# Holding back two decay loads, spreading one norm, joining state masks and moving the mix's scratch in a fused scan and feed-forward kernel

## The chip, the cores and the metric

The kernel runs on one core of a Trainium2 chip, as one launch. The metric is the device time in microseconds (us); lower is better. TensorE (PE) multiplies matrices, VectorE (DVE) and ScalarE (ACT) work elementwise, GpSimd (POOL) has little to do here, and transfers are issued from two queues: SyncE's (SP) and ScalarE's own. Each engine runs its instructions strictly in the order in which the program gives them.

## What is computed

Three stages follow one another: a decaying linear attention (a scan over the sequence), a gated feed-forward with RMS norm, and a second feed-forward that mixes each token with the one before it.

```python
# stage 1: per batch, head; state carried over the sequence
y_i   = sum_{j<=i} (C_i . B_j) * exp(cum_i - cum_j) * x_j + exp(cum_i) * (C_i . state)
state = exp(cum_last) * state + sum_j exp(cum_last - cum_j) * B_j x_j
# stage 2: x = y as (3072 tokens, 256)
xn = x / sqrt(mean(x*x) + 1e-6) * rms_g
x  = (silu(xn @ w_gate) * (xn @ w_val)) @ w_out          # 256 -> 1536 -> 256
# stage 3: per batch of 768 tokens, prev = the token before
xk, xr = mu_k*x + (1-mu_k)*prev, mu_r*x + (1-mu_r)*prev
out = sigmoid(xr @ w_r) * (relu(xk @ w_k)**2 @ w_v)      # 256 -> 1024 -> 256
```

Sizes: 4 batches, 8 heads, 768 positions, head size 32, state size 16.

## The kernel before

**Tiles.** The sequence is cut into six tiles of 128 positions; a tile holds the 4 batches, so 512 columns. For tile t the loop at L993 runs the first feed-forward (`ffn1`, twelve units of 128 hidden columns) and then, behind it, the second feed-forward of tile t-1 (`ffn2`, eight units). Each product of full precision is three matmuls of rounded parts (`mm3`, L748 to L750). In between, hooks weave in the attention of tile c = t+1, and loads for tile e = t+2. The hook "ab" runs ahead of each unit of `ffn1`, the hook "cd" ahead of each unit of `ffn2`.

**Attention of a tile c > 1.** A tile E of decays per batch (128x1024, 4 buffers) is loaded as factors by `load_e` (L332, on ACT's queue, 512 KB each) and turned into running products by `e_scan` (L501, DVE). `terms` (L425 to L433) builds the factors Bs and Cs of a batch's scores with ACT and DVE, and then loads the inputs Br and Cr of the batch after the next (L418, SP's queue). `masked` multiplies scores by decays (L514). `ch_mul` (L496, DVE) scales Ch, which `load_ch` fetches (L320, SP). `y_four` multiplies all out (L594, L527, L533), copies the result yT with ACT, and updates the state (`st_up` L615) and its masked copy Sf (`sf_up` L620), batch by batch. Right behind it stand the four loads of the E tiles for e. Tile 1 does the same in two halves, by `y_two`.

**The norm.** `rms_sq`, `rms_mm`, `rms_a` form the factors; `rms_b` (L711, L712, L720) spreads them over the rows; `xn_f` (L730) multiplies and `xn_split` rounds into two parts (L140 ACT, L143 DVE). For tile 1 all that is needed before its first `ffn1` unit.

**The mix.** `mix` (L809) needs a scratch tile p1 twice per tile. It has the tag "wt", one buffer, which the converted weights of every second pair and, from tile 2 on, the unit output sl use too. The tag "Cs", one buffer too, is that of the terms Cs and of the other converted weights.

**Order.** The program's text gives only ranks. `arrange` (L1357) runs a list scheduler over all instructions with a cost for each, gives each engine the instruction of the lowest rank that is ready and whose buffers are free, and fixes that order. Buffers of a tag are given out in the order in which the text first touches them (`can`, L1265). Instructions under `soonest` are urgent: nothing long is started right ahead of them. `chains` adds an edge of order between two instructions. Weights are converted during tiles 0 and 1 (L268 to L289), on DVE and ACT.

**Semaphores of transfers.** The framework hands eight completion semaphores to the transfers in turn, over both queues, and a transfer waits until the eighth before it has landed. At the end of tile 1's `ffn1` the order is Cr, Ch, E, E, x, E, three decay loads, E: the fourth E load is the eighth after Ch.

Of the kernel before, what the change touches and what calls it, by code (L numbers as in the profile page):

```python
# [13 lines left out]
AF = mybir.ActivationFunctionType  # L14
ALU = mybir.AluOpType

P = 128
NB, NH, S, D, N = 4, 8, 768, 32, 16
NC = S // P
# [5 lines left out]
M8 = 8  # L25
# [4 lines left out]


SCORES = ((4, 7), (3, 8), (2, 4, 8, 10))
VALUES = ((5, 7, 8, 10), (4, 6, 9, 11), (9, 10, 11, 12))
SCAN = ({3: (4,)}, {0: (0,), 1: (4, 1), 3: (2,), 5: (3,)})

NEED = ((4, 6, 8, 8, 10, 12, 12, 14, 16, 16, 18, 18, 18),
# [5 lines left out]
LOW_POOL, ON_POOL = (), ()  # L42

SUB_DVE, MIX_UNIT = tuple(range(27)), 9
MEANS = (7, 10)
WARM, COLD, HALVED, FILL = (9,), 11, 2, {('n', 0): 1, ('n', 2): 1}

TABLES = {AF.Ln: "natural_log_exp_and_others", AF.Exp: "natural_log_exp_and_others",
# [29 lines left out]
def tile_kernel(ctx: ExitStack, tc, a_c, x_t, B_t, B_s, C_s, B_p, C_p, C_h, kc,  # L78
# [116 lines left out]

    def decays(a_sb):
        a_r = t2("a_r")[:NC * NR]
        nc.vector.tensor_copy(a_r, a_sb)
        nc.vector.memset(a_r.rearrange("p (h i) -> p h i", h=4)[:, :, 0:1], 0.0)
        nc.sync.dma_start(out=rows4(la_r.rearrange("c b h i -> (c b h i)")), in_=a_r)  # L200
        nc.sync.dma_start(out=rows4(la_d.rearrange("c b h i -> (c b h i)")), in_=a_sb)
# [127 lines left out]

    def load_e(c, b):  # L330
        e = A[c]["E", b] = rp.tile([P, NH, P], F32, tag="E", bufs=4, name="E")
        nc.scalar.dma_start(  # L332
            out=e.rearrange("p h i -> p (h i)"),
            in_=la_r[c, b].rearrange("h i -> (h i)").unsqueeze(0).broadcast_to([P, NH * P]),
        )

# [224 lines left out]
    def y_two(c, b):  # L563
        d = A[c]
        y = [patt.tile([P, T], F32, tag="at", name="y") for _ in range(2)]
        for k in range(2):
            for half in range(2):
                g = slice(64 * half, 64 * half + 64)
                mm = nc.tensor.matmul(y[half][:, k * P:(k + 1) * P], Sf[g, b + k].rearrange("p h d -> p (h d)"),
                                 d["Ch"][g, b + k, :], start=k == 0, stop=False, skip_group_check=True)  # L570
                if k + half == 0:
                    groups.append((mm.ins.name, [t.name for t in y]))
        for k in range(2):
            y_x(y, (k * P, k * P), c, b + k, False)
            if c + 1 < NC:
                d["up", b + k] = y[k][:, 2 * P:2 * P + 2 * D]
                y_st(d["up", b + k], c, b + k)
        if b == 0:
            d["yT"] = rp.tile([P, 2, T], F32, tag="yT", bufs=1, name="yT")
        for half in range(2):  # L580
            nc.scalar.copy(d["yT"][:, half, b * P:(b + 2) * P], y[half][:, :2 * P])
        for k in range(2):
            st_up(c, b + k)
            sf_up(c, b + k)

    def y_four(c):
        d = A[c]
        y = [patt.tile([P, T], F32, tag="at", name="y") for _ in range(2)]
        more = c + 1 < NC
        u = pmm.tile([P, T], F32, tag="mm", name="u") if more else None  # L590
        for b in range(NB):
            for half in range(2):
                g = slice(64 * half, 64 * half + 64)
                mm = nc.tensor.matmul(y[half][:, b * P:(b + 1) * P], Sf[g, b].rearrange("p h d -> p (h d)"),  # L594
                                      d["Ch"][g, b, :], start=b == 0, stop=False, skip_group_check=True)
                if b + half == 0:
                    groups.append((mm.ins.name, [t.name for t in y + [u] * more]))
        for b in range(NB):
            y_x(y, (b * P, b * P), c, b, False)
            if more:  # L600
                d["up", b] = u[:, 2 * D * b:2 * D * (b + 1)]
                y_st(d["up", b], c, b, True)
        d["yT"] = rp.tile([P, 2, T], F32, tag="yT", bufs=1, name="yT")
        for half in range(2):
            nc.scalar.copy(d["yT"][:, half], y[half])
        for b in range(NB):
            st_up(c, b)
            sf_up(c, b)

    def st_up(c, b):  # L610
        if c + 1 >= NC:
# [3 lines left out]
        nc.vector.scalar_tensor_tensor(out=st, in0=st, scalar=A[c]["la"][:, b, P:P + 1], in1=u,  # L615
                                       op0=ALU.mult, op1=ALU.add)

    def sf_up(c, b):
        if c + 1 < NC:
            nc.vector.tensor_mul(  # L620
                Sf[:, b].rearrange("p (h j) d -> p h j d", j=2),
                state[:, b].unsqueeze(1).broadcast_to([P, NH // 4, 2, D]),
                k_sb[:, M8:M8 + NH // 2].rearrange("p (h j) -> p h j", j=2).unsqueeze(3).broadcast_to([P, NH // 4, 2, D]))


    spans = {}
# [182 lines left out]
    def mix(t, x2, he, le):  # L809
        def seq(ap):  # L810
            return ap.rearrange("p (b i) -> p b i", b=NB)

        last, new = carry[0], rp.tile([P, 2, NB], F32, tag="carry", bufs=2, name="carry")
        carry[0] = new

        def mixed(j, m, p1):
            f = t2("xf")
            if t == 0:
                nc.scalar.activation(out=p1, in_=x2[m][:, :, 1:], func=AF.Copy, scale=mu_v[j][:, m:m + 1])
                nc.vector.scalar_tensor_tensor(out=seq(f), in0=x2[m][:, :, :P], scalar=om_v[j][:, m:m + 1],  # L820
                                               in1=seq(p1), op0=ALU.mult, op1=ALU.add)
                return f
            nc.scalar.activation(out=p1, in_=x2[m], func=AF.Copy, scale=mu_v[j][:, m:m + 1])
            nc.vector.scalar_tensor_tensor(
                out=seq(f)[:, :, 1:], in0=seq(x2[m])[:, :, :P - 1], scalar=om_v[j][:, m:m + 1],
                in1=seq(p1)[:, :, 1:], op0=ALU.mult, op1=ALU.add)
            nc.vector.scalar_tensor_tensor(
                out=seq(f)[:, :, 0], in0=last[:, m, :], scalar=om_v[j][:, m:m + 1],
                in1=seq(p1)[:, :, 0], op0=ALU.mult, op1=ALU.add)
            return f  # L830

        for m in range(2):
            nc.vector.tensor_copy(new[:, m, :], x2[m][:, :, P] if t == 0 else seq(x2[m])[:, :, P - 1])
        for j in range(2):
            p1 = t4("p1")
            fs = [mixed(j, m, p1[:, m, :]) for m in range(2)]
            x = quad("xm")
            for m in range(2):
                xm[t, j, m] = x[:, m]
                split(x[:, m], fs[m], he, le)  # L840

    def ffn2(t, hook):
        acc = [None, None]
# [9 lines left out]
        for u in range(NK):  # L853
            hook("cd", u)
            kp = pmm.tile([P, T], F32, tag="mm", name="kp")
            for k in range(2):
                mm3(kp, wk, k, u, xm[t, 0, k], k == 0, k == 1)
            if u == 0:
                hook("cd2", u)
            rl, k2 = t2("rl"), t2("k2")  # L860
            nc.scalar.activation(out=rl, in_=kp, func=AF.Relu)  # L861
            if t == 0:
                nc.scalar.activation(out=k2, in_=rl, func=AF.Square)
            else:
                nc.vector.tensor_mul(k2, rl, rl)  # L865
            hs[u] = pair("hl", "h2")
            split(hs[u], k2, act_e, vec_e)
            if u >= 3:
                contract(u - 3)
# [123 lines left out]
    for t in range(NC):  # L993
# [11 lines left out]
        def finish(b):  # L1005
            if c > 1:
                if b == NB - 1:
                    y_four(c)
                    for k in range(NB):
                        if e < NC:  # L1010
                            load_e(e, k)
            elif b % 2:
                y_two(c, b - 1)
                for k in range(b - 1, b + 1):
                    if e < NC:
                        load_e(e, k)
# [3 lines left out]
        def attend(u):  # L1020
# [30 lines left out]
            if t == 0:  # L1051
                if u == MEANS[0]:
                    rms_sq(c, cols[0], act_e, vec_e)
                if u == MEANS[0] + 1:
                    rms_mm(c, cols[0])
                if u == MEANS[1]:
                    rms_sq(c, cols[1], act_e, vec_e)
                    rms_mm(c, cols[1])
                    soonest(rms_a, c, full)

        def hook(kind, u):
            if kind == "ab":
                if t == 0:
                    need(NEED[0][u])
                    if u == 0:
                        for b in range(NB):
                            sf_up(0, b)
                if t == 1:
                    need(NEED[1][u])
                    if u == MIX_UNIT:  # L1070
# [7 lines left out]
            if kind == "cd" and c < NC:  # L1078
# [12 lines left out]
                        e_scan(e, 1)  # L1091
                elif u == 6:
                    xn_out(c, (1,), full, act_e, vec_e)

        x2, tail = ffn1(t, hook)
        if t == 0:
            tail()
            hook("ab", NU)
            soonest(rms_b, c, full)
            soonest(xn_out, c, range(2), full, act_e, vec_e)  # L1100
            x2s = quad("x2s", F32).rearrange("p i a n -> p (i a n)")[:, :2 * NB * (P + 1)]
            x2s = x2s.rearrange("p (m b i) -> p m b i", m=2, b=NB)
            nc.gpsimd.memset(x2s[:, :, :, 0:1], 0.0)
# [301 lines left out]
```

## Time and profile before

| | us |
|---|---|
| median of 3 runs | 513.17 (512.85 to 513.82) |
| profiled execution | 516.1 |
| its span | 514.1 |
| TensorE busy in the span | 503.5 (98%) |
| VectorE busy | 377.5 (73%) |
| ScalarE busy | 307.1 (60%) |

The profiled execution is 2.9 us longer than the median of the runs, and 2.0 us of its time lie outside the span. The busy time of TensorE counts pipelined matmuls and says little about its pace; what counts is the distance between the starts of two matmuls in the timeline, 0.23 us for a 128x512 one.

### The profile page before, as it was taken

The numbers are of one execution on the slowest core, as the hardware profiler recorded it, in microseconds if no ns is written. First come the engines' busy times: TensorE is split into PE (matmuls) and PEld (weight loads), VectorE is DVE, ScalarE is ACT, GpSimd is POOL, SyncE is SP. The second block draws the span as 40 slices with busy tenths as digits, with TensorE's granted clock in tenths as the row PEclk, the third lists the DMA queues.
The fourth block names the chain that finished last, engine by engine and source line by source line (L and its number), as shares of the span: only waits on it lengthen the run. The fifth ranks groups of instructions, "written<-read, shape, count | busy, mean of one in ns | idle before, by whom it ended". The sixth has DMA issues, their size and how long they took to land.

```text
span 514.1 us, 7506 instructions
## 1 busy us (share of the span) xinstructions
PE 503.5 (98%) x2869; PEld 407.6 (79%) x2869; DVE 377.5 (73%) x625; ACT 307.1 (60%) x508; POOL 9.5 (2%) x26
## 2 busy tenths in 40 slices
PE   8999999999979999999999999999999999999996
PEld 4687777888858888888888888888888888888885
DVE  6899999979689783759995659996537763335662
ACT  5997778568369753556763546754448642246551
POOL 1000000000010000010000010000001000000000
PEclk9999999999989999999999999999999999999999
DMA  7958565342440111161102143001000010000101
GB/s 258 283 161 271 167 238 195 115 133 83 96 170 0 63 42 41 45 221 63 41 22 82 42 145 122 22 23 40 0 1 1 0 41 3 0 1 0 41 1 41
DMA packets 23283, 42.60 MB, mean 83 GB/s; under 512 B 3136, under 2 KB 6720, under 8 KB 23248
## 3 DMA queue, kind: packets, MB, share of 16 engines
q1 hardware_dynamic: 20496, 33.41, 19.6%
q10 hardware_dynamic: 2752, 8.72, 5.2%
q8 instruction: 22, 0.36, 0.3%
q14 instruction: 13, 0.11, 0.1%
HBM read 38.52 MB, written 3.34 MB: 81 GB/s over the span
## 4 chain that ended last, share of the span: by engine, by line
PE 87%; DVE 7%; DMA 3%; ACT 1%; issue 1%; DVEq 0%; ACTq 0%
PE v L748 10%; PE v L749 10%; PE v L750 10%; PE g L748 6%; PE g L749 6%; PE x L748 6%; PE g L750 6%; PE x L749 6%; PE x L750 5%; PE kp L748 4%; PE kp L749 4%; PE kp L750 4%; PE y L527 2%; DMA Ch<-in_C_h 2%; PE sc L476 1%; DMA E<-la_r 1%
## 5 line engine op out<-in xcount | busy, mean ns | idle before, releaser
L792 DVE TENSOR_TENSOR hf<-sl,v 128x512 f32<-128x512 f32 x72 | 49.1, 684 | 48.2 <-PE v L750 46.9
L140 ACT CAST h<-hf 128x512 fp32r<-128x512 f32 x72 | 44.2, 618 | 64.0 <-DVE hf L792 63.8
L133 ACT ACTIVATE sl<-g 128x512 f32<-128x512 f32 x72 | 42.5, 593 | 46.5 <-PE g L750 40.7
L143 DVE TENSOR_TENSOR h<-hf,h 128x512 fp32r<-128x512 f32 x72 | 50.3, 702 | 26.7 <-ACT h L140 26.6
L748 PE MATMUL x<-h,woh 128*128 128x512 f32 x144 | 56.7, 397 | 3.5 <-ACT h L140 3.1
L748 PE MATMUL g<-xn,wgh 128*128 128x512 f32 (+1 forms) x148 | 57.9, 391 | 0.3 <-ACT wgh L288 0.2
L748 PE MATMUL v<-xn,wvh 128*128 128x512 f32 (+1 forms) x148 | 56.9, 384 | 0.5 <-ACT sl L133 0.5
L749 PE MATMUL x<-h,wol 128*128 128x512 f32 x144 | 56.9, 395 | 0.4 <-DVE wol L289 0.4
L749 PE MATMUL g<-xn,wgl 128*128 128x512 f32 (+1 forms) x148 | 57.0, 385 | 0.0
L749 PE MATMUL v<-xn,wvl 128*128 128x512 f32 (+1 forms) x148 | 56.9, 384 | 0.0
L750 PE MATMUL g<-xn,wgh 128*128 128x512 f32 (+1 forms) x148 | 56.8, 384 | 0.0
L750 PE MATMUL v<-xn,wvh 128*128 128x512 f32 (+1 forms) x148 | 56.8, 384 | 0.0
L750 PE MATMUL x<-h,woh 128*128 128x512 f32 x144 | 56.1, 394 | 0.0
L140 ACT CAST h<-k 128x512 fp32r<-128x512 f32 x48 | 29.7, 620 | 17.8 <-DVE k L865 17.6
L143 DVE TENSOR_TENSOR h<-k,h 128x512 fp32r<-128x512 f32 x48 | 32.8, 687 | 10.0 <-ACT h L140 9.7
L865 DVE TENSOR_TENSOR k<-rl 128x512 f32<-128x512 f32 x40 | 29.1, 727 | 14.9 <-ACT rl L861 14.8
L748 PE MATMUL kp<-xm,wkh 128*128 128x512 f32 x96 | 38.0, 396 | 0.0
L749 PE MATMUL kp<-xm,wkl 128*128 128x512 f32 x96 | 37.6, 392 | 0.0
L750 PE MATMUL kp<-xm,wkh 128*128 128x512 f32 x96 | 37.5, 391 | 0.0
L748 PE MATMUL v<-h,wvvh 128*128 128x512 f32 x96 | 37.4, 389 | 0.0
L749 PE MATMUL v<-h,wvvl 128*128 128x512 f32 x96 | 37.3, 389 | 0.0
L501 DVE TENSOR_TENSOR_SCAN E<-E,cmask 128x1024 f32<-128x1024 f32 x16 | 36.6, 2285 | 0.9 <-DMA E<-la_r 0.9
(157 smaller groups left out, 979.6 us busy)
## 6 DMA issues: line engine op xcount, KB each, us to landing
E<-la_r ACTq DMA_DIRECT2D x16, 512.0 KB
x<-in_x_t SPq DMA_DIRECT2D x6, 512.0 KB
wst<-in_w_gate SPq DMA_DIRECT2D x6, 512.0 KB
wst<-in_w_val SPq DMA_DIRECT2D x6, 512.0 KB
wst<-in_w_out SPq DMA_DIRECT2D x6, 512.0 KB
Br<-in_B_s SPq DMA_DIRECT2D x12, 256.0 KB
Cr<-in_C_s SPq DMA_DIRECT2D x12, 256.0 KB
out<-r SPq DMA_DIRECT2D x11, 256.0 KB
```

The costliest lines, as they stand in the source:

```text
L133: one = nc.scalar.activation(out=out, in_=in_, func=func, **kw).ins.name
L140: last[1] = nc.scalar.copy(x[:, 0, :], src).ins
L143: last[0] = le.tensor_tensor(out=x[:, 1, :], in0=src, in1=f32(x[:, 0, :]), op=ALU.subtract).ins
L476: mm = nc.tensor.matmul(banks[j // 2][j % 2][:, k * w:(k + 1) * w], br[g, k * P:(k + 1) * P], cr[g, k * w:(k + 1) * w], start=True, stop=True)
L501: nc.vector.tensor_tensor_scan(out=e, data0=e, data1=cmask, initial=0.0, op0=ALU.mult, op1=ALU.max)
L527: nc.tensor.matmul(y[half][32 * j:32 * j + 32, at[half]:at[half] + P], x[:, b, h * D:(h + 1) * D], m[:, h, :], start=start and at[half] == ...
L748: nc.tensor.matmul(ps[:, s], w[0][:, k, ws], x[:, 0, s], start=first, stop=False, skip_group_check=s.stop - s.start < T)
L749: nc.tensor.matmul(ps[:, s], w[1][:, k, ws], x[:, 0, s], start=False, stop=False, skip_group_check=s.stop - s.start < T)
L750: nc.tensor.matmul(ps[:, s], w[0][:, k, ws], x[:, 1, s], start=False, stop=last, skip_group_check=s.stop - s.start < T)
L792: nc.vector.tensor_mul(hf, sl, v)
L865: nc.vector.tensor_mul(k2, rl, rl)
```

## The change

- `load_e`: behind `y_four` only the loads of batches 0 and 1 are issued. Those of batches 2 and 3 stand ahead of units 3 and 6 of `ffn2`, each behind the last Relu issued before it (`marks`). Still on ACT's queue. Tile 1's `y_two` keeps its loads, two behind each half.
- `mix`: p1 has the tag "Cs" in place of "wt".
- `sf_up`: one instruction for 4 (or 2) batches in place of one for each, behind all the state updates.
- `decays`: the copy of the 48x512 decays is made by ACT in place of DVE.
- Tile 0: the first half of tile 1's attention is finished ahead of unit 6 in place of 7 (`VALUES`), the first squares of the norm stand at unit 6 in place of 7 (`MEANS`), and `rms_b` and `xn_f` ahead of unit 11 (`SPREAD`) in place of behind the last unit; only `xn_split` stays there.

```diff
-VALUES = ((5, 7, 8, 10), (4, 6, 9, 11), (9, 10, 11, 12))
+VALUES = ((5, 6, 8, 10), (4, 6, 9, 11), (9, 10, 11, 12))
-MEANS = (7, 10)
+MEANS, SPREAD, LOAD_E = (6, 10), 11, (3, 6)
     def decays(a_sb):
-        nc.vector.tensor_copy(a_r, a_sb)
+        nc.scalar.copy(a_r, a_sb)
     def y_two(c, b):
         for k in range(2):
             st_up(c, b + k)
-            sf_up(c, b + k)
+        sf_up(c, b, 2)
     def y_four(c):
         for b in range(NB):
             st_up(c, b)
-            sf_up(c, b)
+        sf_up(c, 0, NB)
     def mix(t, x2, he, le):
-            p1 = t4("p1")
+            p1 = t4("p1", tag="Cs")
     def ffn2(t, hook):
-            nc.scalar.activation(out=rl, in_=kp, func=AF.Relu)
+            marks.append(nc.scalar.activation(out=rl, in_=kp, func=AF.Relu).ins.name)
     def finish(b):
                     y_four(c)
-                    for k in range(NB):
+                    for k in range(2):
                         if e < NC:
                             load_e(e, k)
 # ahead of units of ffn1, tile 0
+                if u == SPREAD:
+                    soonest(rms_b, c, full)
+                    for half in range(2):
+                        soonest(xn_f, c, half, full)
 # hook "cd", ahead of unit u of ffn2
+                if u in LOAD_E and e < NC:
+                    chains.append((marks[-1], load_e(e, 2 + LOAD_E.index(u))))
 # behind ffn1 of tile 0
-            soonest(rms_b, c, full)
-            soonest(xn_out, c, range(2), full, act_e, vec_e)
+            for half in range(2):
+                soonest(xn_split, c, half, full, act_e, vec_e)
```

## Rows read from the trace of the kernel before

**Rows 1.** The page: busy time and count of each engine; the chain by engine.
```profile
PE 503.5 (98%) x2869; PEld 407.6 (79%) x2869; DVE 377.5 (73%) x625; ACT 307.1 (60%) x508; POOL 9.5 (2%) x26
PE 87%; DVE 7%; DMA 3%; ACT 1%; issue 1%; DVEq 0%; ACTq 0%
```

**Rows 2.** The chain that ended last, 134 to 147 us: start, length, engine, line.
```profile
134.77 8.05 DMA Ch<-in_C_h
...
143.88 1.28 ACT L125
145.17 1.06 ACT sq L662
...
146.79 0.63 PE x L748
```

**Rows 3.** Timeline of PE: start, length, line, operation, count, idle before and its releaser.
```profile
143.07 0.39 PE L749 MATMUL x<-h,wol 128*128 128x512 f32 x1
143.29 0.39 PE L750 MATMUL x<-h,woh 128*128 128x512 f32 x1
146.79 0.63 PE L748 MATMUL x<-h,woh 128*128 128x512 f32 x1 [3.11 <-ACT h L140]
...
150.54 0.39 PE L748 MATMUL kp<-xm,wkh 128*128 128x512 f32 x1
```

**Rows 4.** Half-microsecond windows: PE busy (count), granted clock, DMA share, GB/s.
```profile
140.50:141.00 0.50, 0.50 (x4) 1.00 0.79 201
141.00:141.50 0.50, 0.50 (x4) 1.00 1.16 451
...
147.50:148.00 0.50, 0.50 (x2) 0.50 0.34 135
```

**Rows 5.** Timeline of ACT: first E issue of tile 0, the same place, one tile later.
```profile
60.00 0.35 ACTq L332 DMA_DIRECT2D E<-la_r  x1
...
134.96 1.46 ACTq L332 DMA_DIRECT2D E<-la_r  x3
...
142.84 0.33 ACTq L332 DMA_DIRECT2D E<-la_r  x1
143.27 0.60 ACT L133 ACTIVATE sl<-g 128x512 f32<-128x512 f32 x1 [5.73 <-DMA Ch<-in_C_h]
...
226.40 0.33 ACTq L332 DMA_DIRECT2D E<-la_r  x1
```

**Rows 6.** Timeline of DVE around the same place, and one tile later.
```profile
133.37 0.76 DVE L430 SCALAR_TENSOR_TENSOR Cs<-Cr,k_sb,Cs 128x512 fp32r<-128x512 f32 x1
...
138.59 0.29 DVE L620 TENSOR_TENSOR Sf<-state,k_sb 128x128 f32<-128x128 f32 x1
142.84 0.69 DVE L496 TENSOR_TENSOR Ch<-Ch,decay 128x512 f32<-128x512 f32 x1 [3.96 <-DMA Ch<-in_C_h]
...
227.47 0.68 DVE L496 TENSOR_TENSOR Ch<-Ch,decay 128x512 f32<-128x512 f32 x1
```

**Rows 7.** Timeline of SP's queue around the same place, and one tile later.
```profile
134.19 0.54 SPq L418 DMA_DIRECT2D Cr<-in_C_s  x1
134.77 0.48 SPq L320 DMA_DIRECT2D Ch<-in_C_h  x1
...
223.03 0.34 SPq L320 DMA_DIRECT2D Ch<-in_C_h  x1
```

**Rows 8.** DVE in tile 0, and its first scan of a loaded E tile.
```profile
39.74 0.41 DVE L198 COPY a_r<-a_sb 48x512 f32<-48x512 f32 x1
...
65.85 2.29 DVE L501 TENSOR_TENSOR_SCAN E<-E,cmask 128x1024 f32<-128x1024 f32 x1 [0.89 <-DMA E<-la_r]
...
86.63 1.40 DVE L730 SCALAR_TENSOR_TENSOR xnf<-yT,k_sb,rb 128x512 f32<-128x512 f32 x2
```

**Rows 9.** PE from tile 0 to tile 1: last product of tile 0, first of tile 1.
```profile
87.57 0.40 PE L750 MATMUL x<-h,woh 128*128 128x512 f32 x1
88.08 0.50 PE L748 MATMUL g<-xn,wgh 128*128 128x512 f32 x1
```

**Rows 10.** Window behind tile 3's `y_four`: PE, PEld, DVE, ACT, POOL busy; clock, DMA, GB/s.
```profile
232.00:252.00 20.00, 20.00 (x90) 16.44 (x89) 20.00 (x30) 14.93 (x24) 0.00 (x0) 1.00 0.08 27
```

More of the change, by code (lines that the diff above doesn't have):

```diff
@@ L331, in load_e @@
         e = A[c]["E", b] = rp.tile([P, NH, P], F32, tag="E", bufs=4, name="E")
-        nc.scalar.dma_start(
+        return nc.scalar.dma_start(
             out=e.rearrange("p h i -> p (h i)"),
             in_=la_r[c, b].rearrange("h i -> (h i)").unsqueeze(0).broadcast_to([P, NH * P]),
-        )
+        ).ins.name
     a4 = t2("a4").rearrange("p (c i) -> p c i", c=4)[:, :2]
@@ L616, in st_up, with sf_up @@
                                        op0=ALU.mult, op1=ALU.add)
-    def sf_up(c, b):
+    def sf_up(c, b, n=1):
         if c + 1 < NC:
             nc.vector.tensor_mul(
-                Sf[:, b].rearrange("p (h j) d -> p h j d", j=2),
-                state[:, b].unsqueeze(1).broadcast_to([P, NH // 4, 2, D]),
-                k_sb[:, M8:M8 + NH // 2].rearrange("p (h j) -> p h j", j=2).unsqueeze(3).broadcast_to([P, NH // 4, 2, D]))
+                Sf[:, b:b + n].rearrange("p b (h j) d -> p b h j d", j=2),
+                state[:, b:b + n].unsqueeze(2).broadcast_to([P, n, NH // 4, 2, D]),
+                k_sb[:, M8:M8 + NH // 2].rearrange("p (h j) -> p h j", j=2).unsqueeze(1).unsqueeze(4).broadcast_to([P, n, NH // 4, 2, D]))
     spans = {}
@@ L840, in mix @@
                 split(x[:, m], fs[m], he, le)
+    marks = []
     def ffn2(t, hook):
@@ L1065, in hook @@
                     if u == 0:
-                        for b in range(NB):
-                            sf_up(0, b)
+                        sf_up(0, 0, NB)
                 if t == 1:
```

## The prediction

> **What bounds the kernel now.** I read the busy times and the shares of the chain first. TensorE is busy 98% of the span and carries 87% of the chain [rows 1]: at nearly every moment the next thing waited for is a matmul, so work that other engines save is worth nothing unless TensorE was waiting for it. The second reading is therefore the chain in order of time, looking for a place where it leaves TensorE. There are two. One is tile 0, where it runs through the conversions on VectorE with small gaps on TensorE. The other is one spot at the end of tile 1's first feed-forward: it hangs 8.05 us on the load of Ch, then on a table load, the squares and a rounding on ScalarE, and comes back to TensorE at 146.79 [rows 2].
>
> The timeline of TensorE prices that spot. From the matmul at 143.29 to the one at 150.54 there are 10 steps (the row at 150.54 is the tenth start after 143.29), and they take 7.25 us [rows 3]. Two neighbours stand 0.22 to 0.23 us apart just before [rows 3], so 10 steps of 0.227 would take 2.27. The loss is 7.25 - 2.27 = 4.98 us: 3.50 - 0.23 = 3.27 of it waiting, the other 1.71 because the granted clock is 0.50 behind the pause, 1.2 in place of 2.4 GHz [rows 4].
>
> Two engines wait for Ch there. ScalarE stands 5.73 us because the fourth E load cannot be issued before Ch has landed, and sl of unit 11 is queued behind it [rows 5]. VectorE stands 3.96 us in the multiplication of Ch, with hf of unit 11 queued behind it [rows 6]. TensorE needs hf, rounded, for its last six x products. Both waits must go for the loss to go.
>
> **Part by part.**
>
> **The held E loads.** ScalarE issues E0 and E1 behind `y_four`; E2 and E3 follow in `ffn2`. This takes away the issue that waits for Ch, so sl of unit 11 is no longer behind it: ScalarE's 5.73 us go. The two loads now stand in ScalarE's queue behind Relus of units 2 and 5, where Ch has long landed; what is queued behind them is the square or rounding of that unit. An issue takes 0.33 us [rows 5], paid before too, so I take 0; the bounds are 0 and 6 x 0.33 = 2.0 us for three tiles.
>
> **The mix's scratch** decides about VectorE's wait. In the kernel before, the terms of tile 3's first batch are built already in tile 1 (Cs written at 133.37 [rows 6]), and the load of Cr that follows them is issued at 134.19, ahead of Ch at 134.77 [rows 7]. With p1 in the one buffer of Cs, the text touches the mix of tile 1 first, so these terms and the load of Cr must wait until that mix is done, in the second feed-forward. Ch then has its queue to itself, as one tile later: there it is issued at 223.03, and the E load that waits for its semaphore goes out at 226.40, so it took at most 3.37 us [rows 5, 7]; its multiplication at 227.47 shows no idle time before it [rows 6]. Without Cr, whose issue takes 0.54 [rows 7], Ch goes out at about 134.3 and lands by 137.7. VectorE's masked state ends at 138.59 + 0.29 = 138.88 [rows 6], so it loses nothing by Ch. Between v of unit 11 and the pause lie 18 matmuls (six kp, twelve x), so v is done by 143.52 - 18 x 0.227 = 139.4, and hf follows by 139.7 to 140.4. Rounded on ScalarE (0.6) behind table load (1.28) and squares (1.06) [rows 2], which start once sl is done, it is there by about 142, before TensorE reaches it at 143.5. The inputs Br and Cr of batch 2, which now load later on SP's queue, are wanted only at unit 6 of the next tile. Saved: 4.98 us, with the clock. Between ends of 0 and 4.98 I take 4.9, since the twin one tile later lost nothing.
>
> The price of it is two Cs multiplications of 0.76 [rows 6] in each of tiles 2 to 4, now later, next to a stretch in which VectorE is busy 20.00 of 20 us [rows 10]. The same stretch loses two scans of 2.29 [rows 8] to the held loads, so VectorE gets lighter there: 1.52 in, up to 4.58 out. I take 0. If the scans stay, the cover is gone and it is up to 3 x 1.52 = 4.6 us.
>
> **The joined state masks.** Four of 0.29 become one of 128x512, 0.69 by the product of Ch, which has that shape [rows 6]: 4 x 0.29 - 0.69 = 0.47 us less of VectorE. In `y_four` VectorE waits around it, so nothing; in tile 0 it lies on a full VectorE.
>
> **The copy of the decays** takes 0.41 us from VectorE [rows 8] in tile 0 and gives about 0.6 to ScalarE, the length of its 128x512 operations [rows 5], which has idle time in tile 0.
>
> **Tile 0's norm.** Between the last product of tile 0 and the first of tile 1 stand 0.51 us in place of 0.23 [rows 9]: a gap of 0.28 behind xnf and its rounding. Moving `rms_b` and both xnf (1.40 [rows 8]) ahead of unit 11 can close it; but it puts 1.40 us ahead of hf of unit 11 on a full VectorE. The earlier half of tile 1's attention brings its E loads forward; their first scan waited 0.89 [rows 8]. Tile 0 together: VectorE gets 0.47 + 0.41 = 0.88 lighter, which TensorE sees only as far as it waited. Bounds: 0.88 + 0.89 + 0.28 = 2.05 saved, 1.40 lost. I take 0.4 saved, nearest the gap of 0.28, which TensorE itself shows.
>
> **Sum.** 4.9 + 0.4 = 5.3 us. The profiled execution ran 516.1 and becomes 510.8, its span of 514.1 becomes 508.8; the median of the runs, 2.9 below that execution and with nothing in it that would touch this spot, goes from 513.17 to 507.9.
>
> **The rivals.**
>
> **Ch still lands late.** The mechanism: the two queues share the transfer engines, and E0 and E1 (1.0 MB) last as long as Ch's flight whether or not two more stand behind them. For it: the rate was 201 GB/s until 141 and 451 right behind [rows 4], as if the queue with the smaller rows had been served beside the other until then. Against it: Cr is no longer ahead, and the twin had the same E loads. If VectorE waits to 142.84 as before, hf follows at once instead of behind sl: 142.84 + 0.69 for Ch, hf 0.69 by the same shape [rows 6], rounding 0.60 as sl [rows 5], so TensorE goes on at 144.8 and not 146.79, 2.0 us won; if the clock then stays up, 1.7 more. Time 509.5 to 511.2, 510.5 taken. The Trainium skill bears on this (DMA: Bandwidth & Descriptors, section "Queues, rings and completion order"): each transfer engine takes turns between the queues that have work, a packet at a time. By that rule alone, holding back loads that stand behind others in the same queue does not speed up the other queue's; the rates of rows 4 agree with it, and this rival is what it would give.
>
> **The held loads become the wait; slower.** Place: units 3 to 7 of `ffn2` in tiles 1, 2 and 3, on VectorE, where a scan is ordered by the scheduler's idea of the landing. An E load issued at 60.00 let its scan start at 65.85 and cost VectorE 0.89 [rows 5, 8]; Ch cost it 3.96 [rows 6]. If a scan stands ahead of its load's landing in each of three tiles with Ch's price and TensorE's 4.98 behind it, 3 x 4.98 - 5.3 = 9.6 more: 522.8. It decides from 5.3 + 1.0 = 6.3 us over three tiles, 2.1 each. Against it: transfers take only 0.08 of their engines in that stretch [rows 10], so the loads are nearly alone there. At half that price, 7.5 more, it is 515.3, which I take.
>
> **It doesn't do what it says.** The scheduler puts everything in a new order; another load may stand ahead of a product in tile 0 or 1, with a loss of the size of the one removed. Then 512.2 to 514.2.
>
> **How the numbers follow.** Forecast 0.62, Ch late 0.20, slower 0.08, no change 0.10. The forecast's own range is 513.17 - 4.98 - 2.05 = 506.1 to 513.17 - 4.9 + 1.40 = 509.7; with the late Ch it reaches to 511.2. The ends are 506.3 and 511.2. What a measurement here can tell from no change is 0.2%, 1.0 us: faster is below 512.1. Faster takes the first two cases and a little of the last, 0.84; within 0.2% 0.07; slower 0.09.
>
> **What would show it.** Right: at the end of tile 1's `ffn1` no wait on Ch on ScalarE or VectorE, no Cr issued ahead of Ch, TensorE at steps of 0.23 through the first units of the second feed-forward, granted clock 1.00 throughout, and one pair of E issues in `ffn2`. The gap between tiles 0 and 1 below 0.28. Wrong: Ch<-in_C_h still in the chain (the first rival); a wait of a scan on E<-la_r from tile 1 on (the second); a pause of TensorE over 1 us anywhere before 140 (the third).

## The result, and the profile after

| | before | after |
|---|---|---|
| median of 4 runs each, taken side by side (us) | 513.25 (512.85 to 513.82) | 508.68 (508.26 to 508.82) |
| ratio of the runs, 95% interval | | 0.9909 [0.9892, 0.9926] |
| profiled execution / its span (us) | 516.1 / 514.1 | 508.6 / 506.6 |

4.57 us are gone where 5.3 were forecast, and 508.7 stands where 507.9 was expected. The medians further below are of all runs of a kernel; runs over 1.5% above its fastest, one each of e3, e6 and a2 among them, are left out of the ratios. The page of the changed kernel has its chain on TensorE for 91% of the span, with 1% of DMA left and no wait for Ch in it (before: 87% and 3% [rows 1]).

```profile
PE 500.2 (99%) x2869; PEld 406.8 (80%) x2869; DVE 375.7 (74%) x610; ACT 307.9 (61%) x509; POOL 10.4 (2%) x26
...
PE 91%; DVE 5%; ACT 2%; issue 1%; DMA 1%; DVEq 0%; ACTq 0%
```

The spot at the end of tile 1's `ffn1`, in the timelines of SP, ACT and DVE of the changed kernel (start, length, engine, line, operation, and in brackets the idle time before it with its releaser):

```profile
132.29 0.34 SPq L320 DMA_DIRECT2D Ch<-in_C_h  x1
...
132.89 0.88 ACTq L332 DMA_DIRECT2D E<-la_r  x2
...
136.27 0.60 ACT L133 ACTIVATE sl<-g 128x512 f32<-128x512 f32 x1 [0.87 <-PE g L750]
...
135.54 0.69 DVE L620 TENSOR_TENSOR Sf<-state,k_sb 128x512 f32<-128x512 f32 x1
136.15 0.68 DVE L496 TENSOR_TENSOR Ch<-Ch,decay 128x512 f32<-128x512 f32 x1
...
137.64 0.69 DVE L792 TENSOR_TENSOR hf<-sl,v 128x512 f32<-128x512 f32 x1 [0.81 <-PE v L750]
```

Ch goes out with no Cr ahead of it, and its product at 136.15 has no idle time before it: the flight, from issue to landing, took at most 3.86 us, against 8.05 on the chain before [rows 2]. sl of unit 11 waits for its own matmul and no longer for a transfer [rows 5]. TensorE's last x products of unit 11, between which the pause of 3.11 us lay [rows 3], now follow at their pace among products of the next feed-forward:

```profile
141.91 0.39 PE L748 MATMUL x<-h,woh 128*128 128x512 f32 x1
142.13 0.39 PE L749 MATMUL x<-h,wol 128*128 128x512 f32 x1
142.36 0.39 PE L748 MATMUL kp<-xm,wkh 128*128 128x512 f32 x1
142.59 0.61 PE L750 MATMUL x<-h,woh 128*128 128x512 f32 x2
```

So the forecast spot is clean. It isn't where all of the time came from, though. I read one mark from each profile for that: the start of the first matmul of `y_four` (L594), which stands near the end of `ffn1` of tiles 1, 2, 3 and 4. The first mark sums up tile 0 and most of tile 1; the first interval holds the stall.

| profiled execution | first mark | to second | to third | to fourth | to the end |
|---|---|---|---|---|---|
| before, as shown above | 133.16 | 88.66 | 79.76 | 79.68 | 132.84 |
| e0, before, a second execution | 133.09 | 85.60 | 79.68 | 79.66 | 132.87 |
| after | 131.09 | 83.81 | 79.58 | 79.61 | 132.51 |
| e1, before + scratch | 132.51 | 83.75 | 79.66 | 79.64 | 132.44 |
| e2, before + held loads | 133.06 | 84.41 | 79.71 | 79.67 | 132.85 |
| e3, before + both | 132.79 | 83.78 | 79.64 | 79.64 | 132.35 |
| e4, after without these two | 131.18 | 87.20 | 83.52 | 80.96 | 132.84 |
| e5, before + joint masks + copy on ACT | 135.03 | 84.45 | 83.76 | 80.96 | 132.40 |
| e6, before + spread norm | 133.05 | 85.44 | 79.72 | 79.90 | 132.79 |
| e7, before + earlier half and squares | 133.65 | 87.85 | 79.72 | 79.93 | 132.35 |
| a1, after without held loads | 131.37 | 84.03 | 82.35 | 79.62 | 132.43 |
| a2, after without scratch | 130.96 | 84.41 | 80.96 | 80.98 | 132.79 |
| a3, after without joint masks | 130.99 | 83.81 | 79.69 | 79.64 | 132.47 |
| a4, e5 with E loads from SP | 134.54 | 83.66 | 80.68 | 80.90 | 132.42 |

From e0 to after, 2.0 us come ahead of the first mark, 1.8 from the stall, 0.15 from the two intervals behind it and 0.36 from the end: 4.3 us of span. Not all of the 2.0 is the change's. The order of the matmuls is the same in both kernels at least until 23 us, and yet the first factor of tile 0's own norm stands 0.36 us earlier in the changed kernel. Timelines of PE, e0 and then after:

```profile
18.14 0.49 PE L720 MATMUL ss<-tiny 128*128 128x128 f32 x2
```

```profile
17.78 0.49 PE L720 MATMUL ss<-tiny 128*128 128x128 f32 x2
```

This start lies between 17.66 (e3, a2) and 18.21 (before) in the executions of the table, and at 18.79 in a4, where the granted clock was 0.50 around it; two executions of the kernel before agree within 0.07, and whether it goes with the kernel or with the execution these runs don't tell. Counted from it, the first mark is 1.64 or 1.65 us earlier than in e0 in all five kernels that have tile 0's new order (after, e4, a1, a2, a3), so I put 1.65 down to tile 0's edits. The 0.36 us at the end lie behind the last matmul, which starts 128.49 us after the fourth mark in both (506.52 in e0, 502.58 in after): none of the products gained them.

### The profile page after: what moved, and what is told of

Read it like the earlier page. It is cut to its first block, busy times and chain, and to the rows that moved or that the text cites. A ratio compares the mean times of both kernels' runs of the same rounds, so it can differ in the third digit from the quotient of the medians.

```text
span 506.6 us, 7497 instructions
## 1 busy us (share of the span) xinstructions
PE 500.2 (99%) x2869; PEld 406.8 (80%) x2869; DVE 375.7 (74%) x610; ACT 307.9 (61%) x509; POOL 10.4 (2%) x26
## 4 chain that ended last, share of the span: by engine, by line
PE 91%; DVE 5%; ACT 2%; issue 1%; DMA 1%; DVEq 0%; ACTq 0%
PE v L748 10%; PE v L750 10%; PE v L749 10%; PE g L748 6%; PE x L748 6%; PE x L749 6%; PE x L750 6%; PE g L749 6%; PE g L750 6%; PE kp L748 4%; PE kp L750 4%; PE kp L749 4%; PE y L527 2%; PE sc L442 1%; PE rps L750 1%; PE rps L749 1%
## 5 line engine op out<-in xcount | busy, mean ns | idle before, releaser
L748 PE MATMUL x<-h,woh 128*128 128x512 f32 x144 | 55.8, 391 | 0.1
L750 PE MATMUL x<-h,woh 128*128 128x512 f32 x144 | 55.2, 389 | 0.0
L863 ACT ACTIVATE rl<-kp 128x512 f32<-128x512 f32 x48 | 28.5, 594 | 14.1 <-PE kp L750 13.4
## 6 DMA issues: line engine op xcount, KB each, us to landing
E<-la_r ACTq DMA_DIRECT2D x16, 512.0 KB
x<-in_x_t SPq DMA_DIRECT2D x6, 512.0 KB
wst<-in_w_gate SPq DMA_DIRECT2D x6, 512.0 KB
wst<-in_w_val SPq DMA_DIRECT2D x6, 512.0 KB
wst<-in_w_out SPq DMA_DIRECT2D x6, 512.0 KB
```

Of the source, the lines that this page charges most:

```text
L748: nc.tensor.matmul(ps[:, s], w[0][:, k, ws], x[:, 0, s], start=first, stop=False, skip_group_check=s.stop - s.start < T)
L750: nc.tensor.matmul(ps[:, s], w[0][:, k, ws], x[:, 1, s], start=False, stop=last, skip_group_check=s.stop - s.start < T)
L863: marks.append(nc.scalar.activation(out=rl, in_=kp, func=AF.Relu).ins.name)
```

## The experiments

**The kernel before, once more.** Theory A: the stall of 4.98 us is there in every execution. Theory B: its size changes from one execution to the next.

> The kernel before, unchanged, profiled a second time: the first profiled execution ran 516.1 us, 2.9 above the median of its timed runs, while that of the changed kernel ran 508.6, its median. Theory A (the loss of 4.98 us at the end of tile 1's first feed-forward is the same in every run): the pause of TensorE there is 3.1 us and the granted clock 0.50 behind it again, span 514. Theory B (its size varies from run to run, and the timed runs have a smaller one): a pause under 2.5 us or no fall of the clock, span 511 to 512.

512.88 us, the span 510.9. The timelines of SP, DVE, ACT and PE at the same place:

```profile
134.42 0.48 SPq L320 DMA_DIRECT2D Ch<-in_C_h  x1
...
140.99 0.69 DVE L496 TENSOR_TENSOR Ch<-Ch,decay 128x512 f32<-128x512 f32 x1 [2.18 <-DMA Ch<-in_C_h]
...
141.41 0.60 ACT L133 ACTIVATE sl<-g 128x512 f32<-128x512 f32 x1 [3.99 <-DMA Ch<-in_C_h]
...
144.95 0.50 PE L748 MATMUL x<-h,woh 128*128 128x512 f32 x1 [1.34 <-ACT h L140]
```

The same two waits, but Ch landed 1.85 us sooner, TensorE stood 1.34 us instead of 3.11, and the granted clock stayed at its upper level behind the pause. Windows of e0, columns as in [rows 10]:

```profile
146.50:147.00 0.50, 0.48 (x3) 0.34 (x3) 0.33 (x2) 0.50 (x2) 0.00 (x0) 1.00 0.46 170
147.00:149.00 2.00, 2.00 (x10) 1.65 (x9) 2.00 (x3) 0.88 (x3) 0.00 (x0) 1.00 0.23 72
```

The interval was 85.60 us instead of 88.66: 3.06 of the 3.2 us by which the two spans differ. Theory B holds for these two executions; the profiled execution was long because of this very spot.

**The scratch and the held loads, alone and together.** e1 makes one line of the change, e2 the held loads, e3 both:

```diff
-            p1 = t4("p1")
+            p1 = t4("p1", tag="Cs")
```

```diff
-                    for k in range(NB):
+                    for k in range(2):
...
+                if u in LOAD_E and e < NC:
+                    chains.append((marks[-1], load_e(e, 2 + LOAD_E.index(u))))
```

> The kernel before with only the mix's scratch p1 moved to the tag Cs; all four E loads still behind the attention's products, and the fourth still the eighth transfer after Ch. Theory A (the load of Cr ahead of Ch makes Ch late): Ch is issued with no Cr ahead, lands within 3.4 us, the fourth E load and the multiplication of Ch wait for nothing over 0.5 us, TensorE does not pause, 5 us less in the profile, ratio about 0.990 to 0.995. Rival (the E loads share the transfer engines with Ch and make it late): Ch takes 6 to 8 us as before, ScalarE waits over 3 us for it, and the time stays within 1 us of before.

> The kernel before with only the E loads of batches 2 and 3 held behind units of the second feed-forward. Cr is still issued ahead of Ch. Theory A: ScalarE's wait of 5.73 us is gone, but Ch still lands about 8 us after its issue and VectorE stands about 4 us in its multiplication; TensorE pauses 1.3 us in place of 3.1, 2.0 us less if the clock falls again and 3.6 if not. Rival (the E loads make Ch late): Ch lands within 5 us, no pause of TensorE, 5 us less.

> The kernel before with both, the scratch in the tag Cs and the two E loads held; nothing of the edits of tile 0. Theory A: no pause of TensorE at the end of tile 1's first feed-forward, 5 us less in the profile, the same as the scratch alone within 0.5 us; the rest of what the whole change brings is tile 0's. Rival (both are needed): the scratch alone brings under half of this.

e1: 510.75 us, ratio 0.9962 [0.9909, 1.0015]; e2: 511.75, 0.9969 [0.9925, 1.0012]; e3: 510.84, 0.9946 [0.9893, 0.9998]. The runs don't tell the three apart; the marks and rows do. SP, ACT's queue and DVE of e1, then SP and DVE of e2:

```profile
133.71 0.34 SPq L320 DMA_DIRECT2D Ch<-in_C_h  x1
...
136.30 0.33 ACTq L332 DMA_DIRECT2D E<-la_r  x1
...
138.15 0.68 DVE L496 TENSOR_TENSOR Ch<-Ch,decay 128x512 f32<-128x512 f32 x1
```

```profile
133.81 0.54 SPq L418 DMA_DIRECT2D Cr<-in_C_s  x1
134.39 0.48 SPq L320 DMA_DIRECT2D Ch<-in_C_h  x1
...
140.66 0.69 DVE L496 TENSOR_TENSOR Ch<-Ch,decay 128x512 f32<-128x512 f32 x1 [1.88 <-DMA Ch<-in_C_h]
```

With the scratch alone Ch flies at most 2.59 us (the fourth E load, the eighth transfer after it, goes out at 136.30), nobody waits for it, and the interval falls to 83.75, the value of the changed kernel. With the held loads alone ScalarE is free (its sl starts at 138.23 in e2, right behind its matmul), but Ch still takes 6.27 us, close to the 6.57 of e0; the interval falls to 84.41, so 1.2 of the 1.85 us. Both together give 83.78, no more than the scratch. The rule of the Trainium skill named in the prediction (DMA: Bandwidth & Descriptors, "Queues, rings and completion order") agrees with e2: holding back loads that stand behind others on their own queue left the other queue's transfer nearly as late. It is a weak test, since of the two held loads only one was in flight beside Ch; the other went out behind Ch's landing anyway.

Why Cr costs so much more than its own issue is in the packets that each queue moved (queue, packets, MB, share of 16 engines; q1 is SyncE's queue, q10 ScalarE's). First the kernel before from 137 to 141, then e1 from the issue of Ch at 133.71 to 136:

```profile
q10 hardware_dynamic: 149, 0.57, 66.8%
q1 hardware_dynamic: 190, 0.36, 34.1%
```

```profile
q1 hardware_dynamic: 144, 0.26, 38.4%
q10 hardware_dynamic: 44, 0.18, 19.7%
```

In e1 all 0.26 MB of Ch have gone through by 136, when the E loads have moved 0.18. In the kernel before SyncE's queue has 0.52 MB to move, Cr and then Ch; it had moved 0.13 by 137, and most of the rest went side by side with the E loads. So both count: Cr pushes Ch back by a quarter of a megabyte, and thereby into the traffic of the E loads, which is the first rival's mechanism.

**All edits but these two.** e4 has the joint masks, the copy on ScalarE and tile 0's new order.

> The kernel before with all edits but the scratch and the held loads: joint masks, the copy on ScalarE, the earlier half attention and squares, the norm spread ahead of unit 11. Theory A (tile 0 brings 2.0 us of the whole change by itself): the first product with the state in tile 1's feed-forward starts at 131.1 in place of 133.1, and Ch still lands about 6.5 us after its issue at the end of tile 1, with a pause of TensorE of 1 us or more there. Rival (the gain ahead of 131 hangs on the scratch): 132.5 or later.

518.32 us, ratio 1.0111 [1.0085, 1.0137]: 1.1% more than before, clear of the noise. The first mark is 1.9 us earlier, as in the changed kernel, but every interval behind it is longer. Something in these edits makes later tiles slower, and the two others take it away again. Three runs split e4; e5 has the first two edits (of the masks, the line in `y_four` is shown), e6 and e7 one each of tile 0's:

```diff
-            sf_up(c, b)
+        sf_up(c, 0, NB)
...
-        nc.vector.tensor_copy(a_r, a_sb)
+        nc.scalar.copy(a_r, a_sb)
```

```diff
+                if u == SPREAD:
+                    soonest(rms_b, c, full)
+                    for half in range(2):
+                        soonest(xn_f, c, half, full)
...
-            soonest(rms_b, c, full)
-            soonest(xn_out, c, range(2), full, act_e, vec_e)
+            for half in range(2):
+                soonest(xn_split, c, half, full, act_e, vec_e)
```

```diff
-VALUES = ((5, 7, 8, 10), (4, 6, 9, 11), (9, 10, 11, 12))
+VALUES = ((5, 6, 8, 10), (4, 6, 9, 11), (9, 10, 11, 12))
-MEANS = (7, 10)
+MEANS = (6, 10)
```

> The kernel before with only the joint state masks and the copy of the decays on ScalarE: 0.88 us less of VectorE in tile 0. Theory A (TensorE in tile 0 waits for VectorE, so it gets about half of that): that product starts at 132.6 to 132.8. Rival (the waits of TensorE are elsewhere, nothing comes back): 133.0 to 133.2. Rival two (a new order costs something): later than 133.3.

> The kernel before with only the norm of tile 1 spread ahead of unit 11. Theory A (it closes the gap of 0.28 between tiles 0 and 1 and the 0.17 ahead of it): that product starts at 132.6 to 132.8. Rival (two products of 0.7 ahead of hf of unit 11 cost more than the gap): 133.3 to 134.5. Rival two (the order that it makes possible is worth more than the gap): before 132.3.

> The kernel before with only the first half of tile 1's attention and its squares one unit earlier. Theory A (the E loads of tile 2 start earlier, and the wait of 0.89 us of VectorE for the first of them goes): that product starts at 132.2 to 132.8. Rival (that wait was covered): 133.0 to 133.2.

e5: 519.29 us, ratio 1.0139 [1.0097, 1.0181]; e6: 512.38, 1.0005 [0.9977, 1.0033]; e7: 514.72, 1.0050 [1.0025, 1.0075]. So in tile 0 no part helps by itself: counted from the start at L720, the first mark of e5, e6 and e7 is 2.0, 0.0 and 0.95 us later than e0's, while all together (e4) are 1.64 earlier. In e5 the norm still stands at the end of tile 0, and TensorE waits for it:

```profile
89.39 0.50 PE L748 MATMUL g<-xn,wgh 128*128 128x512 f32 x1 [1.81 <-ACT xn L140]
```

What e5 does to later tiles is the main find. The timeline of ACT behind tile 3's `y_four`, in the second interval, then a window of ten microseconds there (columns as in [rows 10]):

```profile
221.28 1.96 ACTq L332 DMA_DIRECT2D E<-la_r  x3
...
226.66 0.33 ACTq L332 DMA_DIRECT2D E<-la_r  x1
227.03 1.06 ACT L662 ACTIVATE sq<-yT 128x1024 f32<-128x1024 f32 x1 [2.67 <-DMA E<-la_r]
```

```profile
225.00:235.00 10.00, 9.17 (x39) 6.69 (x38) 6.48 (x7) 5.66 (x10) 1.29 (x1) 1.00 0.66 213
```

ScalarE stands before the fourth E load. By the order of the eight completion semaphores this load now waits for the first E load of the same burst: with joint masks the state's update ends sooner, so all four of SyncE's decay loads, and not three, take their turns ahead of the fourth E load, and the eighth transfer before it is no longer Ch but one of 512 KB issued 5.4 us earlier (at 221.28). That it is the masks and not the copy, which e5 has too, is read from this order; no run parts the two. TensorE gets 39 matmuls done in that window; in ten microseconds at its full pace the changed kernel does 45 (windows below). A second wait belongs to the mix (timelines of DVE and ACT, in the third interval; TensorE waits 0.92 us for the sl behind it):

```profile
334.25 2.28 DVE L501 TENSOR_TENSOR_SCAN E<-E,cmask 128x1024 f32<-128x1024 f32 x1
...
338.23 1.39 DVE L824 SCALAR_TENSOR_TENSOR xf<-x,om,p 128x508 f32<-128x508 f32 x2
...
339.79 1.14 ACT L140 CAST xm<-xf 128x512 fp32r<-128x512 f32 x2 [3.46 <-DVE xf L827]
```

A decay scan at 334.25 is ordered ahead of the mix's second half on VectorE, and sl of the next units, which has the buffer "wt" too, must wait until the mix has let go of its scratch. Theory T from here on: the held loads take away the first wait, the scratch the second, and the masks are what makes the first necessary. Theory B: one of the two edits does it all, the other is idle.

**One edit taken out of the changed kernel each.** a1 issues all four E loads behind `y_four` again, a2 puts p1 back, a3 masks each batch's state by itself (the line in `y_four` is shown, `y_two` likewise).

```diff
-                    for k in range(2):
+                    for k in range(NB):
...
-                if u in LOAD_E and e < NC:
-                    chains.append((marks[-1], load_e(e, 2 + LOAD_E.index(u))))
```

```diff
-            p1 = t4("p1", tag="Cs")
+            p1 = t4("p1")
```

```diff
-        sf_up(c, 0, NB)
+            sf_up(c, b)
```

> The changed kernel with all four row decays' loads issued together behind the outputs of four blocks again. The first mark of an output of four blocks, 131.1 us in the changed kernel, should stay within 0.2. Theory T (turn): with joint masks the four decay loads on SyncE take their turns ahead of the fourth row decay's load, which then waits for the first of its own burst to land, with ScalarE standing before it, as in the kernel with the masks and tile 0's copy alone (2.67 us, and 5.57 us with all edits but two). Tiles 1 to 2 and 2 to 3 then take longer than the 83.81 and 79.58 us of the changed kernel, each by 0.5 to 4 us; tiles 3 to 4, where the eighth transfer before the fourth load landed long ago, stay at 79.6; in all 510 to 516 us, with ScalarE waits on a row decay's load in the trace. Theory B (the held loads bring little once the scratch is free): all three intervals within 0.3 us of the changed kernel, 508.5 to 509.5 us in all.

> The changed kernel with the mix's shifted operand back in the FFNs' work buffers. Theory T: the C_s load of the next tile is queued ahead of the C_h load again, which takes about 6.3 us to land instead of under 4.4; VectorE waits for it for about 2 us and TensorE loses 0.6 to 1 there (with only the held loads, 84.41 us against 83.75); in tiles 3 and 4 the units' products wait for the mix, 80.5 to 81 us each instead of 79.6; the end is 0.4 us later. In all 511 to 513 us. Theory B: the held loads alone do the work, tiles 2 to 4 as in the changed kernel within 0.3 us, and 508.5 to 509.5 us in all.

> The changed kernel with one mask for each state again behind the outputs of four blocks (tile 0's joint one kept): 12 more VectorE instructions. Theory T: the joint masks bring nothing by themselves, since VectorE is not what TensorE waits for once the held loads and the free scratch are there: all marks within 0.3 us of the changed kernel, 508.2 to 509.2 us. Theory B: the 0.47 us by which a joint mask is shorter reach the end in each of three tiles: about 1.4 us longer, 510 us.

a1: 512.0 us (510.39 to 513.52), ratio 0.9962 [0.9927, 0.9998] to the kernel before; a2: 512.78 (512.01 to 521.27), 0.9993 [0.9953, 1.0032]; a3: 508.63 (508.53 to 508.72), 0.9896 [0.9834, 0.9957].

a1's second interval is 2.77 us longer than in the changed kernel, its third the same, as theory T has it; its first grew by 0.22 only, less than the 0.5 expected. There sl stood 2.08 us behind the E load, without a pause of TensorE behind it. ACT of a1 behind tile 3's `y_four`, a window of a1, and the same window of the changed kernel:

```profile
222.67 0.33 ACTq L332 DMA_DIRECT2D E<-la_r  x1
223.04 1.06 ACT L662 ACTIVATE sq<-yT 128x1024 f32<-128x1024 f32 x1 [2.84 <-DMA E<-la_r]
```

```profile
225.00:235.00 10.00, 8.74 (x35) 6.01 (x34) 9.86 (x13) 5.84 (x11) 0.47 (x1) 1.00 0.23 73
```

```profile
225.00:235.00 10.00, 10.00 (x45) 8.26 (x45) 10.00 (x14) 7.54 (x13) 0.00 (x0) 1.00 0.16 54
```

TensorE gets 35 matmuls done in place of 45: ten steps of 0.23 us, 2.3 of the 2.77 us. In the changed kernel TensorE does its matmuls without a gap there, so what it loses it can't win back.

a2 shows both waits that the scratch takes away: Ch waits behind Cr again, and in tiles 3 and 4 the mix holds up sl (timelines of SP, DVE, ACT and PE):

```profile
131.71 0.54 SPq L418 DMA_DIRECT2D Cr<-in_C_s  x1
132.29 0.48 SPq L320 DMA_DIRECT2D Ch<-in_C_h  x1
...
138.67 0.69 DVE L496 TENSOR_TENSOR Ch<-Ch,decay 128x512 f32<-128x512 f32 x1 [2.57 <-DMA Ch<-in_C_h]
...
251.92 1.14 ACT L140 CAST xm<-xf 128x512 fp32r<-128x512 f32 x2 [3.46 <-DVE xf L827]
...
253.61 0.50 PE L748 MATMUL g<-xn,wgh 128*128 128x512 f32 x1 [0.92 <-ACT sl L133]
```

0.60, 1.38 and 1.37 us in the three intervals. This wait of the mix, too, is there only because of the masks. It is 3.46 or 3.47 us in the four kernels that have the joint masks and p1 in "wt" (e4, e5, a2, a4), and 1.36 and 1.38 at the same place of e0 and e2, which lose nothing by it. In a3 the mix's second pair of roundings on ScalarE starts 3.69 us after the first, as in e0 (3.67); with the masks joined it starts 5.76 us after it, in the changed kernel as in e5, since VectorE then has a decay scan ahead of the second half of the mix. a3 is the changed kernel within 0.1 us in every interval. The joint masks behind `y_two` and `y_four` bring nothing; they cost nothing either as long as the held loads and the scratch are there.

**Turn or traffic?** In a4, e5's E loads are issued from SyncE: the same bytes, but the one who stands before a load is SyncE, and the fourth load's eighth predecessor landed long ago.

```diff
-        nc.scalar.dma_start(
+        nc.sync.dma_start(
```

> The kernel with the joint masks and tile 0's copy on ScalarE alone (84.45, 83.76 and 80.96 us for tiles 1 to 2, 2 to 3, 3 to 4), with the row decays' loads issued from SyncE instead of ScalarE. The bytes, their number and the moment from which they can go stay; the fourth load now takes its turn behind a transfer that landed long ago, and whatever stands before it is SyncE. Theory T (ScalarE stands before the load for its turn): no ScalarE wait on a row decay's load before y's units, tiles 2 to 3 fall from 83.76 to 81 us or less, tiles 3 to 4 stay near 81 (the mix's wait is left); 515 to 517 us in all. Theory B (the traffic of the burst itself is the price): 83.5 to 84 us for tiles 2 to 3, 519 us in all. A third way: SyncE's queue holds the loads back behind C_s and others, so that they land late: over 84 us in tiles 2 to 3.

512.58 us, ratio 0.9994 [0.9964, 1.0024]; the span is 512.2 us, against 516.6 in e5. The second interval falls from 83.76 to 80.68, the third stays (80.90). ACT and then SP behind tile 3's `y_four`:

```profile
221.43 1.07 ACT L605 COPY yT<-y 128x512 f32<-128x512 f32 x2 [3.07 <-PE y L527]
222.53 1.06 ACT L662 ACTIVATE sq<-yT 128x1024 f32<-128x1024 f32 x1
```

```profile
219.99 3.12 SPq L332 DMA_DIRECT2D E<-la_r  x4
```

The squares follow the copies with no idle time, and all four E loads are issued by 223.1. It was the turn at which ScalarE stood, not the traffic. What is left above 79.7 goes with the mix's wait, 3.46 us in both intervals of a4.

## Why the prediction was right, and where its steps were off

**The scratch.** The step was right in place and mechanism: no Cr ahead of Ch, Ch landed in time, and e1 shows that this line alone empties the spot. The twin one tile later was the right row to go by: the prediction read at most 3.37 us for its flight, e1 shows at most 2.59 and the changed kernel at most 3.86. What the prediction had as a rival, the queues' sharing, worked together with Cr and not in its place. The scratch's price, the two Cs multiplications that move behind the mix, was rightly taken at nothing: VectorE stays full there (10.00 of 10 us from 225 to 235, as in [rows 10]), and the two later intervals are no longer than in e0.

**The size of the stall was wrong.** 4.9 us were taken for it, and e0 to after gives 1.8. The step that failed is the last half-sentence of the sum, that the 2.9 us by which the profiled execution exceeds the median had nothing in them that would touch this spot. In the two executions that were traced they were this spot: 3.06 us of interval. Of 4.98 us, 1.77 were a longer pause and 1.71, by the prediction's own sum, the lower clock behind it; neither is there in e0. A stall that hangs on the landing of a transfer needs a second execution before its length goes into a sum against the median.

**Tile 0 was underestimated.** 0.4 was taken between bounds of 2.05 saved and 1.40 lost; 1.65 came. The gap of 0.28 us between the tiles [rows 9] did close, with the first product of tile 1 at 84.13, among the last of tile 0. The bound held, but the choice of the gap of 0.28 us as the nearest row was the fault. What VectorE is spared (0.88) and the earlier half of the attention don't pay by themselves: e5 and e7 lose 2.0 and 0.95, and the spread norm alone (e6) does nothing. Which two of the three would pay together wasn't run, and how the 1.65 us divide can't be told from these runs, since the parts don't add up.

So a term that was 3.1 too large met one that was 1.25 too small, 0.15 of the later intervals, and 0.72 from ahead of L720 and behind the last matmul, which the change doesn't explain. That makes 4.3 of the spans; the medians differ by 4.57. The total was right in part by luck, the shares weren't. (The lower end of the range is given as 506.3 where its own sum gives 506.1; nothing hangs on it.) What shifts the start and the end stays open: e7 shows both and e5 the end, without the scratch or the held loads.

**"In `y_four` nothing" for the joint masks** holds for the changed kernel (a3), and not by itself: e5's second interval is 4.1 us longer than e0's, 3.1 of them through a change of order among transfers (a4) and the rest with the mix's wait. The prediction priced the masks' instructions only, and overlooked that joining them changes the order of what follows, among the transfers and on VectorE. The held loads, priced by Ch alone, earn their 2.8 us here (a1), and only because the masks are joined: e1 has neither, and its later intervals are 79.66 and 79.64. The scratch's 2.75 us in the second and third intervals (a2) come in the same way: e2 has neither the scratch nor the joint masks, and shows 79.71 and 79.67. The kernel with tile 0's edits and the scratch, but neither held loads nor joint masks behind `y_two` and `y_four`, wasn't run; e1 and a3 speak for the same time.

**The rivals.** "Ch still lands late" is what the held loads alone do (e2), and the scratch takes it away, though the sharing that it named is there. The third rival's mechanism, another load ahead of a product, did occur in e4 and e5 and made them 1.1 and 1.4% slower than before. "The held loads become the wait" didn't occur: the timeline of the changed kernel shows none of its 16 scans of E waiting for a load.

## What to carry to other kernels

When a kernel's transfers share a few completion semaphores in turn, an edit that ends some work sooner can move a load ahead of another and so change which transfer a third one waits for; list the turn order of each burst before and after the edit, and keep loads off the queue of an engine that has products to feed. Price a stall that hangs on a transfer from more than one execution. Test edits inside the whole change as well as alone: here masks that brought nothing made the held loads and, in later tiles, the scratch necessary, and three groups of edits that each lost or did nothing saved 1.65 us together. Compare marks from a point ahead of the edited work: here 0.36 us of the first mark's 2.0 were there already.

## What the runs showed of the hardware that was not expected

The granted clock didn't follow the length of the pause. At this one spot it fell to half (1.2 GHz) behind a pause of 3.11 us in the kernel before [rows 4], stayed at the full 2.4 GHz behind pauses of 1.34 us (e0) and 2.92 us (e4), and fell behind one of 1.73 us, with another 0.25 us at 147.57, in e7. The timeline and a window of e4, then of e7:

```profile
144.62 0.50 PE L748 MATMUL x<-h,woh 128*128 128x512 f32 x1 [2.92 <-ACT h L140]
```

```profile
147.00:148.00 1.00, 1.00 (x6) 0.81 (x5) 1.00 (x3) 0.00 (x1) 0.00 (x0) 1.00 0.01 3
```

```profile
145.90 0.50 PE L748 MATMUL x<-h,woh 128*128 128x512 f32 x1 [1.73 <-ACT h L140]
```

```profile
148.00:149.00 1.00, 1.00 (x4) 0.74 (x3) 1.00 (x3) 0.17 (x1) 0.00 (x0) 0.50 0.29 86
```

e7's first interval is 0.65 us longer than e4's, although its pause is 1.19 us shorter.

The flight of Ch spread too: with Cr ahead it was 8.05 us in one execution of the kernel before, 6.57 at most in the other, and 6.27 and 6.38 at most in e2 and a2, at nearly the same place of the program; without Cr it was at most 3.86 and 2.59 (after, e1).
